# Keeping loads, transposes and small DMAs in program order, with late output weights and two more pattern buffers, in an attention kernel bound by exponentials

## The chip, the cores and the metric

The kernel runs on one core of one Trainium2 chip. The metric is the device time of one execution in microseconds (us), as the median of several executions. The kernel before took 898.3 us as the median of three runs (897.33 to 899.11). The profile of one execution is the source of everything finer than that. Its span is about 2 us shorter than the time of the run: for the kernel before 897.7 of 899.51, so the execution that was profiled is one of its slower ones. The engines go by short names: PE multiplies matrices, ACT, DVE and POOL work on elements, SP issues transfers. SBUF is the memory on the chip, PSUM the memory that PE writes its results to.

## The reference, cut to what matters

Two attention blocks, A and B, each work on 2048 rows of 512 columns with 32 heads of 16 columns, and their results stand side by side in the output.

```python
def _A_ref(x, wq, wk, wv, wo, beta):          # four segments of L = 512 rows
    ...                                        # q, k, v = x @ wq, x @ wk, x @ wv, split by head and segment
    for s in range(N):
        logits = jnp.einsum('bhqd,bhkd->bhqk', qs, ks) * scale + mask
        p = _softmax(logits, axis=-1)
        a_dot = jnp.einsum('bhqk,bhkd->bhqd', p, vs)
        pq = phi(qs)
        a_mem = ...                            # from the memory M, z of the segments before
        o = g * a_mem + (1.0 - g) * a_dot
        M = M + jnp.einsum('bhld,bhle->bhde', phi(ks), vs)
        z = z + ...
    return o @ wo

def _B_ref(x, wqkv, wo):                       # full attention over 2048 rows
    scores = jnp.einsum('bhqd,bhkd->bhqk', q, k) * Dh ** (-0.5)
    p = _softmax(scores, axis=-1)
    ...
    return o @ wo
```

Part A works on one segment after another: each needs its slice of `x`, transposed, then projections to `q`, `k` and `v`. Part B has 2048 by 2048 scores for each head, sixteen times those of one segment of A, and so most of the exponentials.

## The kernel before

ACT computes exponentials (`pT`) from score tiles that PE writes into PSUM (`s_ps`). DVE takes 500 of part B's 2048 score tiles (`v_ps`) in another way: it writes bit patterns into buffers named `vx` ("pattern buffers", 10 of them), which serve as probabilities directly; four such tiles make a block. PE multiplies both kinds by the values into `acc`. SP issues nearly all transfers, one after another.

A segment of A's input is loaded by four transposes into a buffer that exists once. The query of a unit of work (one segment of rows and one quarter of the heads) is projected into `q_ps`, cast by DVE to `qc`, and spread by head parity into `qa` (part A) or `qb` (part B): by eight small copies that SP issues when the plan finds SP free, or by two POOL instructions otherwise.

```python
    def load_xT(pool, name, ch, tag, bufs):
        t = pool.tile([P, 4, W], BF16, name=f"xT_{name}", tag=tag, bufs=bufs)
        for cc in range(4):
            nc.sync.dma_start_transpose(t[:, cc, :], xs[name][ch * W:(ch + 1) * W, cc * P:(cc + 1) * P])
        return t
    ...
        def evac():                                    # in do_q, the query projection
            qc = wk.tile([P, W], BF16, name="qc", tag="qc", bufs=2)
            pin(nc.vector.tensor_copy(qc[:], ps[:]))
            if live[0] and T["sp"] < T["dve"] + 1.0:
                for e in range(2):
                    for j in range(4):
                        r = slice(32 * j + DH * e, 32 * j + DH * e + DH)
                        nc.sync.dma_start(out=dst[r, e, :], in_=qc[r, :])
                        on_sp(0.5, T["dve"] + 0.1)
                mark(key, T["sp"] + 2.2)
            else:
                ...                                    # two POOL instructions
```

`pin` keeps an instruction where the program has it; what is not pinned may be moved by the scheduler that comes after. In the kernel before the matmuls and the work of DVE, ACT and POOL are pinned and the transfers are not.

The program plans its own order while it is written out. `T` holds a planned clock for each engine (`T["pe"]`, `T["sp"]` and so on), and the work beside the score tiles consists of "chores", each with a due place and perhaps an earliest time `after` and a condition `ok`. A chore starts only once its `after` has passed on PE's planned clock.

```python
        def startable(c):
            return ((c["after"] is None or c["after"] <= T["pe"]) and (c["ok"] is None or c["ok"]())
                    and (not c["slot"] or free_slots(T["pe"] + 0.05)))
        ...
        def seg_chores(s, rt):                         # for segment s of A and each quarter rt of the heads
            ...
            def project():
                rel = T["sp"] + 3.5
                if (s, rt) != (0, 0):
                    chore(d - LEAD, part(k()), 4, after=rel if s else ARRIVE["w1" if rt == 1 else "wk"],
                          key=("k", "a", s, rt), ok=lambda: s == 0 or ("phk", s - 1, rt) in seen)
                    chore(d - LEAD, part(q()), 4, after=rel if s else ARRIVE["w1" if rt == 1 else "wq"],
                          key=("q", "a", s, rt))
                ...
            def load():
                if s > 0:
                    xTA[s] = load_xT(wk, "a", s, "xTA", 1)
                    on_sp(4 * 1.3, T["pe"])
                ...
                project()
            if rt == 0:
                chore(d - 18, load(), 1, slot=False, ok=...)
            else:
                project()
        ...
        def unit_done(u):
            ...
            if name == "a" and ch < NSEG - 1:
                mem_chores(ch, rt)
                seg_chores(ch + 1, rt)
```

For the first quarter, `project()` is called by `load()`, so its `rel` ("the time at which the load has landed, by plan") is right. For the other quarters it is called when a unit of the segment before is done, and that can be before the load has been planned: `rel` is then a time already past.

## Time and profile before

| | kernel before |
|---|---|
| time, median of 3 runs | 898.3 us |
| span of the profiled execution | 897.7 us |
| ACT busy | 866.6 us, of it 747 exponentials with 854.9 us |
| ACT idle: first 20 us / 180 to 200 / 880 to the end / elsewhere | 8.67 / 7.30 / 10.36 / 4.74 us |

The page of a profile gives the busy time of each engine and the costliest groups of instructions. A group's row reads: line, engine, operation, output from input, count; then busy time and the mean of one in ns; then how long the engine was idle just before them and what ended most of that. Since ACT's idle time is the only thing that can shrink as long as its work stays the same, it is worth listing by stretches. The DMA issues of the kernel before, with count, size of each and median time from issue to landing, name the transfers that the change touches:

```profile
qb<-qc SPq DMA_DIRECT2D x96, 16.0 KB, 1.8
qa<-qc SPq DMA_DIRECT2D x72, 16.0 KB, 1.8
wo_a<-in_A_wo_dram SPq DMA_DIRECT2D x1, 512.0 KB, 5.0
```

So 21 query splits (168 copies in eights) go over SP's queue, and the output weights take 5.0 us to land.

### The profile page before, as it was taken

The page shows a single profiled execution, that of the slowest core. Times are in us where ns is not written, and L with a number is a line of the kernel's source. Part 1 is how long each engine was busy: PE and PEld are TensorE (multiplying, and loading weights), DVE is VectorE, ACT ScalarE, POOL GpSimd, SP SyncE. Part 2 cuts the span into 40 slices and gives each one's busy share as a digit, 9 for nine tenths or more (in the row PEclk, how much of TensorE's full clock was granted, in tenths as well). Part 3 has the DMA queues.
Part 4 walks back from the last instruction along what each step waited for, and adds up shares of the span by engine and source line. Part 5 has one row for each costly group of instructions (what it writes and reads, how often), then busy time and mean ns, then how long its engine had stood idle before and what let it go on. Part 6 is the DMA issues. An engine that isn't in the chain of part 4 may idle for free.

```text
span 897.7 us, 19235 instructions
## 1 busy us (share of the span) xinstructions
PE 863.9 (96%) x7673; PEld 258.9 (29%) x7673; DVE 796.1 (89%) x1362; ACT 866.6 (97%) x777; POOL 130.8 (15%) x295
## 2 busy tenths in 40 slices
PE   9999999979999999999999999999999999999996
PEld 3322332312323232222232322323222322222222
DVE  4786699959998998989989999999999999999994
ACT  6999999969999999999999999999999999999995
POOL 7710300310202003030110302002030300000000
PEclk9999999979999999999999999999999999999998
DMA  9600000200001201000000210000000000000000
GB/s 194 140 10 12 24 18 9 48 18 7 15 6 19 60 23 28 7 7 13 2 19 2 42 37 12 3 1 7 1 8 1 19 24 13 1 2 1 1 2 29
DMA packets 48181, 19.85 MB, mean 22 GB/s; under 512 B 37200, under 2 KB 48080, under 8 KB 48080
## 3 DMA queue, kind: packets, MB, share of 16 engines
q1 hardware_dynamic: 46736, 17.99, 9.1%
q8 instruction: 62, 1.02, 0.5%
q10 hardware_dynamic: 1344, 0.52, 0.2%
q14 instruction: 39, 0.32, 0.1%
HBM read 4.20 MB, written 4.19 MB: 9 GB/s over the span
## 4 chain that ended last, share of the span: by engine, by line
ACT 25%; PE 21%; issue 9%; DVE 5%; POOL 0%; DVEq 0%; ACTq 0%
ACT pT L893 24%; PE acc L117 11%; PE s_ps L117 6%; PE v_ps L117 2%; DVE vx L966 2%; DVE vx L982 2%; PE o_ps L117 1%; DVE tT L382 1%; ACT ex L307 0%; POOL pT L903 0%; PE l_ps L117 0%; PE q_ps L117 0%; DVE OT_b L430 0%; DVE rsum L405 0%; DVE osb L1264 0%
## 5 line engine op out<-in xcount | busy, mean ns | idle before, releaser
L893 ACT ACTIVATE pT<-s_ps 128x1536 bf16<-128x1536 f32 x747 | 854.9, 1289 | 13.0 <-PE s_ps L117 8.8
L966 DVE TENSOR_SCALAR vx<-v_ps 128x512 uint16<-128x512 f32 x500 | 328.4, 685 | 26.8 <-PE v_ps L117 21.6
L117 PE MATMUL s_ps<-qb,KB 32*128 32x512 bf16 x1548 | 249.4, 384 | 8.2 <-ACT pT L893 4.0
L982 DVE TENSOR_SCALAR vx<-vx 128x2048 uint16<-128x2048 uint16 x375 | 248.9, 693 | 5.0 <-PE v_ps L117 3.2
L117 PE MATMUL v_ps<-qb,KB 32*128 32x512 bf16 x500 | 181.8, 382 | 2.0 <-DVE vx L966 0.9
L117 PE MATMUL acc<-vx,VB 128*32 128x512 f16 x2000 | 180.8, 384 | 2.0 <-DVE vx L982 0.7
L903 POOL TENSOR_SCALAR_AFFINE_SELECT pT<-pT 128x256 bf16<-128x256 bf16 (+2 forms) x241 | 105.8, 469 | 481.8 <-ACT pT L893 481.3
L117 PE MATMUL acc<-pT,VB 128*32 128x512 bf16 x1548 | 151.6, 389 | 0.0
L117 PEld LDWEIGHTS <-KB 32*128 32x128 bf16 x2048 | 82.8, 91 | 237.1 <-issue 230.2
L117 PE MATMUL acc<-zeros 128*128 128x512 bf16 x395 | 135.4, 389 | 0.0
L117 PEld LDWEIGHTS <-VB 128*32 128x32 bf16 x3548 | 73.4, 94 | 165.6 <-issue 154.1
L117 PE MATMUL s_ps<-qa,kA 32*128 32x384 bf16 (+3 forms) x512 | 53.3, 299 | 5.3 <-ACT pT L893 3.0
L117 PEld LDWEIGHTS <-zeros 128*128 128x128 bf16 x417 | 34.2, 98 | 82.5 <-issue 77.2
L382 DVE STREAM_TRANSPOSE tT<-acc 128x512 f32<-128x512 f32 x64 | 44.9, 704 | 12.8 <-PE acc L117 12.4
L117 PE MATMUL acc<-pT,vA 128*32 128x256 bf16 (+3 forms) x512 | 33.3, 306 | 0.3 <-POOL pT L903 0.2
L117 PEld LDWEIGHTS <-kA 32*128 32x128 bf16 x512 | 17.8, 91 | 45.3 <-issue 42.3
L272 DVE CAST qc<-q_ps 128x512 bf16<-128x512 f32 x28 | 19.1, 684 | 6.8 <-PE q_ps L117 6.6
L117 PE MATMUL q_ps<-xT_a,w_a 128*128 128x512 bf16 x64 | 19.8, 386 | 5.0 <-DMA xT_a<-in_A_x_dram 5.0
L460 DVE CAST osb<-o_ps 128x512 bf16<-128x512 f32 x28 | 19.1, 683 | 4.6 <-PE o_ps L117 4.1
L416 POOL TENSOR_TENSOR tN<-tT,rsum 128x512 bf16<-128x512 f32 x1 | 1.4, 1368 | 130.1 <-DVE rsum L405 130.1
L117 PE MATMUL k_ps<-xT_a,w_a 128*128 128x512 bf16 x64 | 19.8, 398 | 0.0
L117 PE MATMUL o_ps<-wo_a,OT_a 128*128 128x512 bf16 x64 | 18.8, 383 | 0.3 <-DVE vx L966 0.2
(94 smaller groups left out, 409.7 us busy)
## 6 DMA issues: line engine op xcount, KB each, us to landing
out_dram<-osb SPq DMA_DIRECT2D x30, 128.0 KB, 1.7
w_b<-in_B_wqkv_dram SPq DMA_DIRECT2D x3, 512.0 KB, 6.0
qb<-qc SPq DMA_DIRECT2D x96, 16.0 KB, 1.8
qa<-qc SPq DMA_DIRECT2D x72, 16.0 KB, 1.8
phk<-phkT SPq DMA_TRANSPOSE x48, 2.4
w_a<-in_A_wv_dram SPq DMA_DIRECT2D x1, 512.0 KB, 5.1
wo_a<-in_A_wo_dram SPq DMA_DIRECT2D x1, 512.0 KB, 5.0
wo_b<-in_B_wo_dram SPq DMA_DIRECT2D x1, 512.0 KB, 4.9
```

The lines of the kernel that those rows point to most:

```text
L117: return pin(nc.tensor.matmul(out, lhsT, rhs, **k))
L272: pin(nc.vector.tensor_copy(qc[:], ps[:]))
L382: pin(nc.vector.transpose(st["tT"][:, e].rearrange("p c d -> p (c d)"), acc[:]))
L416: pin(eng.tensor_tensor(o, tT[:, :, :, 0:DH], rr.to_broadcast(bc), op=ALU.mult))
L460: pin(nc.vector.tensor_copy(osb[:], ps[:]))
L893: pin(nc.scalar.activation(pT[:, 0:n, :], pt[:, 0:n, :], ACT.Exp, scale=SCALE))
L903: pin(nc.gpsimd.affine_select(out=blk, in_=blk, compare_op=ALU.is_ge, fill=0.0, base=0, pattern=[[0, len(sls)], [1, P]], channel_multiplie ...
L966: pin(nc.vector.tensor_scalar(x[:, j, :], vt[:], XSCALE, float(LADDER[0]), ALU.mult, ALU.add))
L982: pin(nc.vector.tensor_scalar(p[:], x[:], float(off - LADDER[0]), 32767.0, ALU.add, ALU.min))
```

## The change

The intent, as read from the diff, is to remove the hole at 180 to 200 us and to use SBUF better. Every transfer is pinned, so that SP issues in the order of the program. The output weights no longer occupy buffers of their own from the start: they are loaded later into two of the pattern buffers, and these become 12 in place of 10, so that two more are there early.

```diff
-VBUFS = 10
+VBUFS = 12
...
-    def load_wo(pool, name, eng):
-        t = pool.tile([P, NRT, D], BF16, name=f"wo_{name}", tag=f"wo_{name}")
-        eng.dma_start(out=t[:], in_=wos[name].rearrange("(rt p) n -> p rt n", p=P))
+    def load_wo(pool, name, tag, bufs):
+        t = pool.tile([P, NRT, D], BF16, name=f"wo_{name}", tag=tag, bufs=bufs)
+        pin(nc.sync.dma_start(out=t[:], in_=wos[name].rearrange("(rt p) n -> p rt n", p=P)))
...
-            nc.sync.dma_start_transpose(t[:, cc, :], xs[name][ch * W:(ch + 1) * W, cc * P:(cc + 1) * P])
+            pin(nc.sync.dma_start_transpose(t[:, cc, :], xs[name][ch * W:(ch + 1) * W, cc * P:(cc + 1) * P]))
...
-                        nc.sync.dma_start(out=dst[r, e, :], in_=qc[r, :])
+                        pin(nc.sync.dma_start(out=dst[r, e, :], in_=qc[r, :]))
...            (the same pin on the loads of weights and beta, the phk transposes and the output)
-        woA = load_wo(big, "a", nc.sync)
-        woB = load_wo(big, "b", nc.sync)
+        wo = {}
...
+        def wo_loads():
+            for name in "ab":
+                vlive[0] += 1
+                wo[name] = load_wo(wk, name, "vx", VBUFS)
+                on_sp(0.55, T["pe"])
+            wo["at"] = T["sp"] + 4.0
+            return
+            yield
+        chore(60, wo_loads(), 1, slot=False, ok=lambda: vlive[0] + 2 < VBUFS and place() > 40)
...
-                    chore(at + 8 + 4 * sb, do_out(mp, wk, name, ot, woA if name == "a" else woB, ch, sb, gone))
+                    chore(at + 8 + 4 * sb, do_out(mp, wk, name, ot, wo, ch, sb, gone),
+                          ok=lambda: wo.get("at", 1e9) < T["pe"])
```

More of the change, by code (lines that the diff above doesn't have):

```diff
@@ L191, in load_beta @@
     def load_beta():
-        nc.sync.dma_start(out=beta_a[:], in_=A_beta.partition_broadcast(P))
+        pin(nc.sync.dma_start(out=beta_a[:], in_=A_beta.partition_broadcast(P)))
     def spread_beta():
@@ L221, in load @@
         def load(eng, i, lo=0, hi=D):
-            eng.dma_start(out=t[i][:, :, lo:hi],
-                          in_=srcs[i][:, lo:hi].rearrange("(cc p) n -> p cc n", p=P))
+            pin(eng.dma_start(out=t[i][:, :, lo:hi],
+                              in_=srcs[i][:, lo:hi].rearrange("(cc p) n -> p cc n", p=P)))
         return t, load
-    def load_wo(pool, name, eng):
-        t = pool.tile([P, NRT, D], BF16, name=f"wo_{name}", tag=f"wo_{name}")
-        eng.dma_start(out=t[:], in_=wos[name].rearrange("(rt p) n -> p rt n", p=P))
+    def load_wo(pool, name, tag, bufs):
+        t = pool.tile([P, NRT, D], BF16, name=f"wo_{name}", tag=tag, bufs=bufs)
+        pin(nc.sync.dma_start(out=t[:], in_=wos[name].rearrange("(rt p) n -> p rt n", p=P)))
         return t
@@ L337, in move @@
             for kb in range(4):
-                nc.sync.dma_start_transpose(ph[:, kb, :], pk[:, kb * P:(kb + 1) * P])
+                pin(nc.sync.dma_start_transpose(ph[:, kb, :], pk[:, kb * P:(kb + 1) * P]))
             on_sp(4 * SPTRANS, T["dve"] + 0.1)
@@ L451, in do_out @@
     def do_out(mp, wk, name, ot, wo, ch, sb, then=None):
+        if isinstance(wo, dict):
+            wo = wo[name]
         ps = palloc(mp, [P, D], "o_ps")
@@ L461, in evac @@
             r0 = ch * W + sb * P
-            nc.sync.dma_start(out=out2[r0:r0 + P, col0[name]:col0[name] + D], in_=osb[:])
+            pin(nc.sync.dma_start(out=out2[r0:r0 + P, col0[name]:col0[name] + D], in_=osb[:]))
             on_sp(0.55, T["dve"] + 0.1)
@@ L1227, in partial @@
             for rt in range(NRT - 1):
-                mm(t, ot[:, rt, sb * P:(sb + 1) * P], woB[:, rt, :], start=(rt == 0), stop=False,
+                mm(t, ot[:, rt, sb * P:(sb + 1) * P], wo["b"][:, rt, :], start=(rt == 0), stop=False,
                    skip_group_check=True)
@@ L1248 @@
                                     tN[:, 4 * sb:4 * sb + 4, :].rearrange("p c d -> p (c d)")))
-            mm(ps[sb], ot[:, NRT - 1, sb * P:(sb + 1) * P], woB[:, NRT - 1, :], start=False, stop=True,
+            mm(ps[sb], ot[:, NRT - 1, sb * P:(sb + 1) * P], wo["b"][:, NRT - 1, :], start=False, stop=True,
                skip_group_check=True)
@@ L1293, in exact_problem @@
                 ld(nc.sync, i)
-            wo = load_wo(big, name, nc.sync)
+            wo = load_wo(big, name, "wo", 1)
             xT = [load_xT(big, name, ch, f"xT{ch}", 1) for ch in range(4)]
```

## The prediction

> **What bounds the kernel now.** I read the page's busy line first, then the row of the costliest group, then all engines in stretches of 20 us, and last the one stretch that stood out, in 2 us steps and in order of time.
>
> ```profile
> PE 863.9 (96%) x7673; PEld 258.9 (29%) x7673; DVE 796.1 (89%) x1362; ACT 866.6 (97%) x777; POOL 130.8 (15%) x295
> L893 ACT ACTIVATE pT<-s_ps 128x1536 bf16<-128x1536 f32 x747 | 854.9, 1289 | 13.0 <-PE s_ps L117 8.8
> ```
>
> ACT is busy 866.6 of 897.7 us, 854.9 of it in the 747 exponentials `pT`. PE at 96% is partly filler (395 matmuls on `zeros`). So the span is ACT's work plus ACT's idle time. The stretches say where that lies (columns: stretch, PE, PEld, DVE, ACT, POOL busy, granted clock, DMA share, GB/s):
>
> ```profile
> 160.00:180.00 20.00, 19.17 (x175) 6.71 (x173) 18.90 (x37) 20.00 (x19) 8.58 (x19) 1.00 0.27 53
> 180.00:200.00 20.00, 14.96 (x92) 3.35 (x92) 10.19 (x18) 12.70 (x13) 3.67 (x4) 0.74 0.09 20
> 200.00:220.00 20.00, 19.47 (x174) 5.78 (x174) 19.61 (x34) 19.66 (x19) 0.00 (x0) 1.00 0.03 8
> ```
>
> Over all stretches ACT's idle time is 8.67 us in the first 20 us, 7.30 in 180 to 200, 10.36 from 880 to the end, and 4.74 spread over the other 840 us. With 866.63 busy that is the 897.7. So only 7.3 us lie in one hole, and PE, DVE and ACT all stop in it. What stops them, by the waits and the time line:
>
> ```profile
> PE q_ps L117 <- DMA xT_a<-in_A_x_dram: 5.0, 1, 5.0
> 174.84 3.74 SPq L234 DMA_TRANSPOSE xT_a<-in_A_x_dram  x3
> 178.68 4.96 SPq L277 DMA_DIRECT2D qa<-qc  x8
> 180.30 0.82 PE L117 MATMUL q_ps<-xT_a,w_a 128*128 128x512 bf16 x3
> 183.68 1.26 SPq L234 DMA_TRANSPOSE xT_a<-in_A_x_dram  x1
> 186.48 0.59 PE L117 MATMUL q_ps<-xT_a,w_a 128*128 128x512 bf16 x1 [5.04 <-DMA xT_a<-in_A_x_dram]
> 188.63 1.45 ACT L893 ACTIVATE pT<-s_ps 128x1536 bf16<-128x1536 f32 x1 [5.02 <-PE s_ps L117]
> ```
>
> The four transposes that load the third segment of A's input (`xT_a`) stand in SP's queue as three, then eight small copies `qa<-qc` of the query split, then the fourth. PE does three matmuls of a query projection, then waits for the fourth transpose, and everything behind it in PE's order waits too. The clock falls as well:
>
> ```profile
> 186.00:188.00 2.00, 1.52 (x12) 0.17 (x11) 0.89 (x2) 0.00 (x0) 0.11 (x1) 0.50 0.00 0
> 192.00:194.00 2.00, 2.00 (x9) 0.24 (x6) 0.49 (x1) 0.63 (x2) 0.00 (x0) 0.50 0.10 17
> 194.00:196.00 2.00, 2.00 (x19) 0.49 (x18) 1.90 (x5) 1.95 (x2) 0.00 (x0) 0.80 0.09 16
> ```
>
> So the hole is 5.02 us without matmuls plus about 2.3 us (7.30 - 5.02) of small gaps while PE runs at half clock up to about 194.8.
>
> **What the Trainium skill says.** "Perfetto Trace Analysis", Identifying the Most-Contended Engine: occupancy is a fair measure for ACT, matmul busy share is not one for PE; the trace agrees, since ACT's gaps account for the span. The same page, DMA Instruction — HWDGE (DVE, Sync): the sequencer waits for semaphores, generates descriptors, and only then is free; the movement itself lies outside the profiled slice. The trace agrees: a transpose held SP 1.26 us and PE resumed 186.48 - 183.68 = 2.8 us after its start. "DMA: Bandwidth & Descriptors", Issuing engines are not separate DMA queues, calls the sequencer's issue time "usually small relative to the DMA itself"; here it is not: eight `qa` copies hold SP 4.96 us and each lands in 1.8. "TensorE: Matmul & The Clock Gate", What's actually happening: an idle window of about 3.4 us halves PE's clock, and some 3.4 us of sustained work restores it. Here 5.0 us of idleness halved it, but it came back only some 8 us after PE resumed.
>
> **The change, part by part.** (1) ACT and DVE work: counted over the two built programs, both have the same instructions on these engines, 747 exponentials and 125 pattern blocks (500 evacuations) included. The two extra pattern buffers let blocks start earlier, but take nothing off ACT: 0 us of work. (2) Three query splits move from 24 SP copies (-16 `qa`, -8 `qb`) to 6 POOL instructions of 0.7 to 0.9 us; POOL is at 15% and their readers come tens of tiles later: 0. (3) The two output weight loads leave the front of SP's queue (1.44 + 0.51 us of issue at 33.7 to 35.7), where ACT idles only 0.27 us between 20 and 40: at most 0.3 us. Their late place is 8 score tiles ahead of the first reader, some 9 us at 1.14 us a tile (854.9 / 747), against 5.0 us to land: no wait. (4) Program order on SP. This should close the hole, and what matters is what that order is. In the changed program it reads: eight `qa<-qc`, then all four transposes of the third `xT_a`. The last reader of the old `xT_a`, which frees the buffer, is the same matmul whose result the eight copies carry. So the first three transposes lose the place ahead of the copies that the scheduler had given them. And PE's order has the first matmul on the new `xT_a` two score tiles after that last reader; before it came five tiles after, and the one on the fourth transpose six.
>
> Clocked from t = end of that last reader (174.8 before), by durations of the trace:
> - DVE's cast of `qc` ends at 0.8 (before: 175.61); copies 0.9 to 5.9 (4.96); transposes start at 5.9, 7.15, 8.4, 9.65 (1.26 each) and land 2.8 later: 8.7, 9.95, 11.2, 12.45. In the kernel before the four landed at about 2.8, 4.1, 5.3 and 11.6.
> - PE reaches its first matmul on them at about 1.8: two score tiles behind exponentials of 1.36 and 0.95, and eight small matmuls (0.45). It waits 6.9 us. ACT has two exponentials and one `ex` (0.7) in store and runs dry at 3.9, as before 2.15 us after PE stopped (181.46, 183.61).
> - PE's order is two of the four matmuls, a score tile, the other two. The score tile follows the second landing: 9.95 + 0.45 + 0.6 at half clock, ACT resumes at 11.1. Gap 7.15.
> - The next tile waits for the fourth landing, 12.45, one matmul (0.45), twelve column matmuls (1.45 at the pace of 187.00 to 187.97 for eight) and its own 0.6: 14.95, while ACT ended at 12.55. Gap 2.4.
> - Then PE is at half clock and dense with projections: gaps of about 0.45, 0.7 and 0.9, until the clock returns near 18 to 21; I take 1.8 for the three.
>
> Sum 11.4 us of idle ACT in place of 7.3: +4.1. The other five late `xT` loads of the changed program have their first reader 10 tiles or more after the issue, longer than 5.0 + 2.8 us, so no second hole. 898.3 + 4.1 = 902.4 us.
>
> **The rivals.** First, the intent: the order closes the hole. Then 898.3 - 7.3 = 891.0. For it speaks that no copies stand between transposes any more; against it that they now stand ahead of all four. It needs PE to reach the reader some 5 to 10 us later than its order suggests. Second, half of it: PE comes late by a few us because DVE or a buffer holds it, and the longer queue and the shorter wait cancel: 896 to 899. Third, a new wait at the split `qa` of a later unit: its copies now follow the two weight loads, and its first reader comes 8 tiles after its cast (9.2 us, against 4.96 + 1.8 + 0.8). Tight but enough; if a weight load waits for its buffer, up to 3 us more: 905. Fourth, the drift of the 4.74 us of small gaps under a changed interleaving: 2 us either way.
>
> **Range and chances.** Gain beyond 2% means under 880.3, but ACT's work with today's head and tail alone is 866.6 + 8.7 + 10.4 = 885.7: excluded unless the work shrinks, and it doesn't. Loss beyond 2% means over 916.3, that is a second hole of twice the size: unlikely. I give the longer hole 75%, cancelling 12%, the closed hole 8%, worse 5%. Predicted 902.4, range 897 to 907; faster 0.01, same 0.96, slower 0.03.
>
> **What would show it.** Right: in the changed kernel's time line eight `qa` copies end just before four `xT_a` transposes of 1.26 us in a row, near 175 to 186 us; PE `q_ps` waits for the `xT_a` DMA 6 to 8 us in total, in more than one piece; ACT idles 10 to 13 us in the 20 us around it; the exponentials stay at 747 and about 855 us; first and last 20 us are unchanged. Wrong: ACT busy 20 of 20 us there (the closed hole), or a wait of a score tile for `qa<-qc`, or of `o_ps` for the weights, or a DVE or POOL group grown by more than 3 us.

## The result, and the profile after

The changed kernel took 901.12 us (median of four runs, 900.9 to 901.68), against 898.02 us (four runs, 897.33 to 899.11) for the kernel before on the same chip. The ratio is 1.0034, with a 95% interval of 1.0017 to 1.0052. Here and below a ratio is the mean time of one kernel's fast runs over the mean of the other's fast runs of the same rounds, so it is not quite the ratio of the medians quoted; in the experiments below, the first execution of each kernel, the profiled one, is left out of it. All runs quoted here count as fast.

The page of the changed kernel, its busy line and the row of the costliest group:

```profile
PE 850.7 (95%) x7617; PEld 258.8 (29%) x7677; DVE 792.7 (88%) x1362; ACT 866.0 (96%) x777; POOL 131.2 (15%) x301
...
L903 ACT ACTIVATE pT<-s_ps 128x1536 bf16<-128x1536 f32 x747 | 854.2, 1294 | 16.2 <-PE s_ps L117 14.1
```

The work is the same: 747 exponentials, 854.2 us. What changed is the idle time before them, 16.2 us, of which 14.1 ended with a score tile of PE, in place of 13.0 and 8.8. The stretches of the changed kernel (PE, PEld, DVE, ACT, POOL busy, granted clock, DMA share, GB/s) say where:

```profile
160.00:180.00 20.00, 16.31 (x142) 5.84 (x143) 16.47 (x35) 19.08 (x18) 7.65 (x18) 1.00 0.22 37
180.00:200.00 20.00, 14.00 (x72) 3.31 (x73) 5.71 (x10) 10.08 (x10) 4.51 (x6) 0.66 0.15 33
200.00:220.00 20.00, 18.59 (x173) 5.45 (x173) 19.09 (x33) 19.84 (x19) 0.00 (x0) 1.00 0.06 12
```

ACT idles 0.92 + 9.92 = 10.84 us in the first two, where it idled 7.30 before. The mean granted clock of the second stretch is 0.66 in place of 0.74. The row of the waits for the same transfer, and then the time line of the changed kernel around it (start, duration, engine, line, operation, count, and in brackets the idle time before it with what ended it):

```profile
PE q_ps L117 <- DMA xT_a<-in_A_x_dram: 8.5, 4, 6.9
```

```profile
176.29 4.94 SPq L277 DMA_DIRECT2D qa<-qc  x8
181.33 5.12 SPq L234 DMA_TRANSPOSE xT_a<-in_A_x_dram  x4
184.04 0.61 PE L117 MATMUL q_ps<-xT_a,w_a 128*128 128x512 bf16 x1 [6.91 <-DMA xT_a<-in_A_x_dram]
...
186.46 1.45 ACT L903 ACTIVATE pT<-s_ps 128x1536 bf16<-128x1536 f32 x1 [7.38 <-PE s_ps L117]
...
187.97 0.59 PE L117 MATMUL q_ps<-xT_a,w_a 128*128 128x512 bf16 x1 [0.69 <-DMA xT_a<-in_A_x_dram]
...
190.11 1.02 ACT L903 ACTIVATE pT<-s_ps 128x1024 bf16<-128x1024 f32 x1 [1.69 <-PE s_ps L117]
```

The reader should see four things. The eight `qa` copies end just before four transposes in a row. PE waits for each of the four landings, not for one: 8.5 us in 4 waits in place of 5.0 in 1. The first wait begins at 177.1 us, 1.7 us after the last matmul on the old buffer ended (175.47). And ACT's gaps, 7.38, 1.69 and after these 0.49, 1.11 and 0.17, sum to 10.84.

The span grew from 897.7 to 899.2 us. By ACT's idle time the hole gave +3.54, the first 20 us -0.20 (8.47 idle), the stretch from 880 us -0.53 (9.83), all other idle time -0.70 (4.04), and the busy time -0.6: together +1.5. One execution each is profiled, the kernel before in a slower one than its median, as said above; the medians of the runs differ by 3.1.

The transfers, from the DMA issues of the changed kernel:

```profile
qb<-qc SPq DMA_DIRECT2D x88, 16.0 KB, 1.8
qa<-qc SPq DMA_DIRECT2D x56, 16.0 KB, 1.8
```

Three splits have moved to POOL (24 copies fewer), and no row of the waits shows anything waiting for the output weights, which are now issued at about 76 us.

### The profile page after: what moved, and what is told of

It reads as the page before. It is cut to its first block, busy times and chain, and to the rows that moved or that the text cites. A ratio compares the mean times of both kernels' runs of the same rounds, so it can differ in the third digit from the quotient of the medians.

```text
span 899.2 us, 19135 instructions
## 1 busy us (share of the span) xinstructions
PE 850.7 (95%) x7617; PEld 258.8 (29%) x7677; DVE 792.7 (88%) x1362; ACT 866.0 (96%) x777; POOL 131.2 (15%) x301
## 2 busy tenths in 40 slices
DMA packets 47412, 19.45 MB, mean 22 GB/s; under 512 B 36816, under 2 KB 47312, under 8 KB 47312
## 4 chain that ended last, share of the span: by engine, by line
PE 23%; ACT 20%; issue 7%; DVE 4%; DMA 0%; DVEq 0%; SPq 0%; ACTq 0%
ACT pT L903 19%; PE acc L117 13%; PE s_ps L117 7%; PE v_ps L117 2%; DVE vx L976 1%; DVE vx L992 1%; PE o_ps L117 1%; DVE tT L382 0%; PE q_ps L117 0%; DMA phk<-phkT 0%; DMA out_dram<-osb 0%; DVE osb L462 0%; PE l_ps L117 0%; ACT ex L307 0%; DVE tN L428 0%
## 5 line engine op out<-in xcount | busy, mean ns | idle before, releaser
L903 ACT ACTIVATE pT<-s_ps 128x1536 bf16<-128x1536 f32 x747 | 854.2, 1294 | 16.2 <-PE s_ps L117 14.1
L992 DVE TENSOR_SCALAR vx<-vx 128x2048 uint16<-128x2048 uint16 x375 | 245.8, 683 | 2.6 <-PE acc L117 1.2
L117 PE MATMUL v_ps<-qb,KB 32*128 32x512 bf16 x500 | 179.6, 381 | 2.3 <-DVE osb L462 0.6
L913 POOL TENSOR_SCALAR_AFFINE_SELECT pT<-pT 128x256 bf16<-128x256 bf16 (+2 forms) x241 | 102.8, 456 | 532.4 <-ACT pT L903 531.4
L117 PE MATMUL s_ps<-qa,kA 32*128 32x512 bf16 (+3 forms) x512 | 53.2, 299 | 5.7 <-ACT pT L903 3.6
L117 PE MATMUL q_ps<-xT_b,w_b 128*128 128x512 bf16 x53 | 18.2, 410 | 1.1 <-issue 0.7
L117 PE MATMUL k_ps<-xT_a,w_a 128*128 128x512 bf16 x58 | 17.8, 382 | 0.6 <-issue 0.6
```

The lines of the kernel that those rows point to most:

```text
L117: return pin(nc.tensor.matmul(out, lhsT, rhs, **k))
L903: pin(nc.scalar.activation(pT[:, 0:n, :], pt[:, 0:n, :], ACT.Exp, scale=SCALE))
L913: pin(nc.gpsimd.affine_select(out=blk, in_=blk, compare_op=ALU.is_ge, fill=0.0, base=0, pattern=[[0, len(sls)], [1, P]], channel_multiplie ...
L992: pin(nc.vector.tensor_scalar(p[:], x[:], float(off - LADDER[0]), 32767.0, ALU.add, ALU.min))
```

## The experiments

Each was run in five rounds, and all results were correct. The theory (A): the hole comes from the plan, which lets PE start a query projection on an input segment right behind the last reader of the old one, without knowing that the new one is not there; the rest of the change sets only how long that wait is: what stands ahead of the transposes in SP's queue, and how soon PE's order comes to the projection. The rival at first (B): SP's order alone made the difference. A second one (C): part of the later gaps is the granted clock, not the transfer.

### The changed kernel again

No edit; it gives the spread against the same runs of the kernel before that the next three are compared with.

> The changed kernel once more, on the same chip as the other runs of this call. All theories: about 901 us, ratio to the kernel before 1.002 to 1.005, ACT idle 10 to 11.5 us between 160 and 200 us (it was 10.84 in its first trace, 7.30 in the kernel before).

Measured: 901.54 us (899.7 to 902.02) against 897.52 (9 runs), ratio 1.0038 [1.0024, 1.0052]. The hole in its profile is 1.11 + 9.37 = 10.48 us. The result repeats, with some 0.4 us of scatter in the hole. This profile also has 1.95 us of idle ACT at 510 to 530 us, where the first profile of the kernel had 0.45.

### Order alone

The kernel before with `pin` around every transfer, and nothing else:

```diff
-            nc.sync.dma_start_transpose(t[:, cc, :], xs[name][...])
+            pin(nc.sync.dma_start_transpose(t[:, cc, :], xs[name][...]))
...            (and so for the copies, loads and outputs)
```

> The kernel before with program order on SP's queue alone: old buffers, old weight loads. The built program equals the kernel before on PE, DVE, ACT and POOL; only SP's order differs (eight copies, then all four transposes of the third xT_a). Theory A (what costs is how far behind the last reader PE reaches the new xT_a, and that is set by the interleaving, not by the queue): PE still comes five to six tiles after the last reader, so it waits about 3 us for the first and 1 to 2 for the others; hole 7.5 to 8.5 us, time 897.5 to 900. Rival B (the order of the queue alone makes the whole loss): hole about 11 us, 901 to 902. Rival C (the intent: program order on the queue closes the hole): under 893.

Measured: 898.47 us (897.62 to 900.48) against 897.52, ratio 1.0013 [0.9999, 1.0027]. The time line of this run:

```profile
175.03 4.94 SPq L277 DMA_DIRECT2D qa<-qc  x8
180.07 5.12 SPq L234 DMA_TRANSPOSE xT_a<-in_A_x_dram  x4
...
186.59 1.02 ACT L893 ACTIVATE pT<-s_ps 128x1024 bf16<-128x1024 f32 x1 [4.50 <-PE s_ps L117]
```

SP's order is that of the changed kernel, and PE's program is that of the kernel before. Three of the four transposes now start some 5 us later (the first at 180.07 in place of 174.84), and yet the hole is 6.95 us, no larger than 7.30 (and below the 7.5 to 8.5 expected). PE waits 4.5 us in three pieces in place of 5.0 in one. The last transpose leaves SP at 180.07 + 5.12 = 185.19 us, and in the kernel before at 183.68 + 1.26 = 184.94: what ends the hole is the end of the whole sequence of copies and transposes, and that hardly depends on the order within it (counted from the end of the last reader, 174.21 us here and 174.82 before, it is 0.9 us later). Rivals B and C are out: order alone neither closes the hole nor brings the whole loss. It does not show any loss for certain, since its interval includes 1, but one of up to 0.27% is not excluded.

### Buffers and late weights alone

The changed kernel with `pin` taken off every transfer, so the scheduler may again move them.

```diff
-            pin(nc.sync.dma_start_transpose(t[:, cc, :], xs[name][...]))
+            nc.sync.dma_start_transpose(t[:, cc, :], xs[name][...])
...            (and so for the others)
```

> The changed kernel without program order on its transfers: twelve pattern buffers and late weights stay. The built program equals the changed one on PE, DVE, ACT and POOL; SP's order is two transposes, eight copies, two transposes. Theory A: PE comes two tiles after the last reader, gets the first two transposes after a short wait, then waits for the third and fourth; hole about 10 to 11 us in two pieces, the first about 1 us and the second about 7.5; time 900 to 901.5. Rival B: hole as in the kernel before, 7.3 us, 898. A third view, that the buffers help by themselves: under 897.

Measured: 899.27 us (897.95 to 900.38), ratio 1.0018 [1.0005, 1.0032]. From its time line:

```profile
178.26 4.97 SPq L280 DMA_DIRECT2D qa<-qc  x8
183.28 2.56 SPq L237 DMA_TRANSPOSE xT_a<-in_A_x_dram  x2
...
189.55 1.02 ACT L906 ACTIVATE pT<-s_ps 128x1024 bf16<-128x1024 f32 x1 [7.07 <-PE s_ps L120]
```

The scheduler again puts transposes ahead of the copies, but only two of the four, at 175.73 us. PE waits 0.95, 5.64 and 0.78 us. The hole is 0.68 + 8.67 = 9.35 us, a little below the 10 to 11 that I expected, and so is the time. The new interleaving of PE's work is therefore the larger part of the growth of the hole: +2.05 us without the order, and 1.1 to 1.5 us more with it (10.48 and 10.84). The times don't settle the shares: 1.0018 here and 1.0013 for order alone have intervals that overlap. This run holds both the two early buffers and the late weights; which of them moved PE's order is not separated.

### The reader told when the load has landed

The changed kernel with a correction of the plan alone. A projection may not start before its load has been planned, and its earliest time is set to the planned landing:

```diff
-        u_at, nmem, nproj = [0], {}, {0: 2}
+        u_at, nmem, nproj, xin = [0], {}, {0: 2}, {0: 0.0}
...
-                          key=("k", "a", s, rt), ok=lambda: s == 0 or ("phk", s - 1, rt) in seen)
+                          key=("k", "a", s, rt), ok=lambda: s in xin and (s == 0 or ("phk", s - 1, rt) in seen))
...
-                          key=("q", "a", s, rt))
+                          key=("q", "a", s, rt), ok=lambda: s in xin)
...
                     on_sp(4 * 1.3, T["pe"])
+                    xin[s] = T["sp"] + 3.5
+                    for c in chores:
+                        if c["key"] is not None and c["key"][1:3] == ("a", s):
+                            c["after"] = xin[s]
```

> The changed kernel with one correction in the kernel's own planner: the k and q projections of a later segment are held until the time planned for that segment's xT_a load, in place of a time taken before the load was planned. SP's order stays (copies, then four transposes); the first reader of the third xT_a moves from two score tiles after the last reader to fourteen. ACT and DVE have the same instructions. Theory A: no wait for the xT_a transfer, hole under 1 us, clock stays at 1.0; time 901.1 - 10.8 + up to 1 = 890 to 891.5, faster than both kernels. Rival (the loss is not this wait, the time only moves to another one): 897 or more.

Measured: 890.56 us (890.31 to 892.87), ratio 0.9925 [0.9911, 0.9938] to the kernel before. Its stretches:

```profile
160.00:180.00 20.00, 18.81 (x162) 6.60 (x163) 16.69 (x36) 20.00 (x19) 7.66 (x18) 1.00 0.21 37
180.00:200.00 20.00, 19.19 (x163) 6.27 (x167) 17.68 (x29) 20.00 (x20) 3.15 (x4) 1.00 0.17 37
```

ACT is busy 20.00 of 20 us in both, at full clock, and no wait for `xT_a` is left. SP's order is unchanged: the copies at 176.29 us and the four transposes at 181.34, almost to the hundredth where they were in the changed kernel. So nothing had to be done about the queue; the transfer had been early enough for the work, and only the place of the projections in PE's order was wrong. This is the strongest run for theory A. The two parts of the correction, the condition and the new time, were tested together. A second buffer for `xT_a`, which would let the load start before the last reader is done, was not tried.

### The copies twice

In the changed kernel, the eight copies of that one query are issued twice; the planned cost of each is halved, so that the plan stays as it was.

```diff
-                for e in range(2):
+                for e in [0, 1] * (2 if key == ("q", "a", 1, 3) else 1):
...
-                        on_sp(0.5, T["dve"] + 0.1)
+                        on_sp(0.25 if key == ("q", "a", 1, 3) else 0.5, T["dve"] + 0.1)
```

> The changed kernel with the eight copies ahead of the third xT_a load issued twice (the same data to the same place; result unchanged, all other engines' programs equal). Theory A: the four transposes start 8 x 0.62 = 4.96 us later, PE waits 11.9 us for the first, and the whole of it goes into the time: hole 15.5 to 16.5 us, time 905.5 to 907. Rival (SP's issue time lies beside other work, the wait is for the movement of the data): under 903.

Measured: 905.69 us (905.35 to 906.15) against 898.14 (11 runs), ratio 1.0083 [1.0068, 1.0098]. In the time line:

```profile
175.97 10.00 SPq L277 DMA_DIRECT2D qa<-qc  x16
186.07 5.12 SPq L234 DMA_TRANSPOSE xT_a<-in_A_x_dram  x4
...
191.34 1.45 ACT L903 ACTIVATE pT<-s_ps 128x1536 bf16<-128x1536 f32 x1 [12.58 <-PE s_ps L117]
```

The hole is 16.0 us. Another 5.06 us of issue made the first gap 5.2 us longer (12.58 in place of 7.38) and left the later ones nearly alone (1.60, 0.49, 1.33, 0.32). Issue time ahead of the transposes goes into the time one for one, or nearly: the ratios differ by 0.0045 to 0.0049 from the changed kernel's, which is 4.0 to 4.4 us.

### No copies

In the changed kernel, that one query is split by two POOL instructions in place of eight copies, with the plan's clock for SP unchanged.

```diff
-                        pin(nc.sync.dma_start(out=dst[r, e, :], in_=qc[r, :]))
+                        if key != ("q", "a", 1, 3):
+                            pin(nc.sync.dma_start(out=dst[r, e, :], in_=qc[r, :]))
+                        elif j == 0:
+                            pin(nc.gpsimd.tensor_scalar(dst[:, e, :], qc[:], par[:, e:e + 1], 0.0, ALU.mult, ALU.add))
```

> The changed kernel with no copies ahead of that load: this one query split is done by two POOL instructions, the plan's clocks are left as they were, so PE, DVE and ACT have the same programs. Theory A: the transposes start at the last reader's end and land 2.8, 4.1, 5.3 and 6.6 us after it, PE at 1.8 waits about 1 us three times; hole 2.5 to 4.5 us, time 893 to 895. If only the late plan of the reader counted and not the queue, the hole would stay over 7 us and the time over 897.

Measured: 895.1 us (894.79 to 896.05), ratio 0.9968 [0.9955, 0.9982]. From its time line and its stretches:

```profile
176.13 5.12 SPq L234 DMA_TRANSPOSE xT_a<-in_A_x_dram  x4
180.00:200.00 20.00, 18.22 (x112) 4.65 (x113) 10.90 (x18) 15.78 (x15) 4.52 (x6) 0.83 0.10 21
```

PE waits 3.6 us in four pieces of at most 1.4. ACT's gaps are 1.78, 1.79, 0.49, 0.65 and 0.17, 4.88 us in all, a little more than the 2.5 to 4.5 expected; the clock fell here too (mean 0.83). The hole shrank by 6.0 us against the changed kernel, and the ratios differ by 6 us too. So even with a free queue the plan's mistake costs some 4 to 5 us (the hole, and 0.9968 against 0.9925): a transpose took 1.26 us to issue and nearly 3 to land.

### The correction in the kernel before

The correction above in the kernel before, with nothing else.

> The kernel before with the planner's correction alone: old queue order, ten pattern buffers, early weights. The planner then gives one block less to DVE (124 of 125), so ACT has two exponentials of 2 banks more, about 1.9 us. Theory A: 898.0 - 7.3 + 1.9 = 892.6, between 891.5 and 894; so most of the gain needs neither the program order nor the buffers. Rival (the order on the queue is needed for it): over 896.

Measured: 895.38 us (894.26 to 896.14), ratio 0.997 [0.9956, 0.9984]. This is a miss: I had expected 892.6. The hole at 180 to 200 us is gone (19.93 us busy of 20), but a second one has come at 500 to 520 us:

```profile
500.00:520.00 20.00, 15.14 (x134) 4.00 (x137) 14.66 (x28) 14.97 (x15) 0.00 (x0) 0.91 0.21 56
505.49 0.69 DVE L460 CAST osb<-o_ps 128x512 bf16<-128x512 f32 x1 [4.08 <-DMA out_dram<-osb]
```

SP had two transposes, eight `qb` copies and two more transposes in its queue, and then four outputs; DVE waited 4.08 us for the buffer of one output (`osb`). The plan also came out with 749 exponentials in place of 747 (124 pattern blocks and not 125), but their busy time, 854.7 us, is that of the kernel before within 0.3 us, so it is not this that was lost. The correction changes the whole plan, and what closing the old hole gave was mostly spent again in the new one.

### The correction without the order

The corrected changed kernel with `pin` taken off the transfers.

> The corrected changed kernel without program order on its transfers (programs of PE, DVE, ACT, POOL equal to the corrected one). Theory A: the reader comes fourteen tiles, some 16 us, after the last reader, so either order of the queue is in time: 890 to 891.5, same as with order. Rival (program order is worth something by itself once the reader is told): 892 or more.

Measured: 891.26 us (889.46 to 892.22), ratio 0.9922 [0.9907, 0.9938]: the same as with the order. With the reader told, program order on SP is worth nothing measurable in this kernel.

### The correction and the order, with the old buffers

The kernel before with the pins and the correction: whether the order closes the second hole of the correction in the kernel before, where copies stood between transposes.

> The kernel before with the planner's correction and program order on SP's queue, but ten pattern buffers and early weights: the programs of PE, DVE, ACT and POOL equal those of the corrected kernel with the old rest (895.4), only SP's order differs. That kernel had a second hole of about 5 us near 500 us, where output transfers stood behind a split load (two transposes, eight copies, two transposes) and DVE waited 4.1 us for an output buffer. Theory: program order puts the outputs at their planned place, that hole goes: 890 to 892. Rival (that hole belongs to the plan of the other engines, not to the queue): 894 or more.

Measured: 896.06 us (895.51 to 897.72) against 897.65 (11 runs), ratio 0.9984 [0.9972, 0.9996]. A miss for the theory that the order would close it; the rival held. From the time line, SP and DVE:

```profile
493.74 5.46 SPq L277 DMA_DIRECT2D qb<-qc  x8
499.30 5.12 SPq L234 DMA_TRANSPOSE xT_b<-in_B_x_dram  x4
504.54 3.09 SPq L462 DMA_DIRECT2D out_dram<-osb  x4
...
506.58 0.69 DVE L460 CAST osb<-o_ps 128x512 bf16<-128x512 f32 x1 [4.42 <-DMA out_dram<-osb]
```

Three outputs that DVE had ready in their buffers at 496.9 to 501.6 us stand behind 10.7 us of copies and transposes (493.74 to 504.42); there are three `osb` buffers, the next output has none, and DVE, pinned in its order, stops for 4.42 us. In the corrected changed kernel the same stretch has the outputs between the other transfers (two at 498.47 us, right after the copies) and ACT busy 19.98 of 20 us. So the rest of the change is worth something after all, some 5 us by the two ratios (0.9925 and 0.9984), but by another plan of the work near 500 us, not by the order.

### The first wait filled

The changed kernel with 28 matmuls on zeros (which add nothing) in front of the waiting projection, so that PE does not idle there.

```diff
+                if (s, rt) == (2, 1):
+                    for _ in range(28):
+                        pin(nc.tensor.matmul(accs[cur[0]][:], zeros[:, 0, :], zcols, start=False, stop=False,
+                                             skip_group_check=True))
                 yield from do_q(...)
```

> The changed kernel with 28 more zero matmuls of 0.216 us (about 6.0 us) just before the first matmul that waits for the third xT_a, the plan's clocks left as they are: PE works where it waited, so its clock should not be halved. Theory: the wait for the transfer stays (first ACT gap about 6.9 us in place of 7.4), but the gaps after it, 3.5 us in the changed kernel, fall to about 1; granted clock 1.0; hole 7.5 to 8.5 us; time 898 to 899.5. Rival (the later gaps come from the order of the work and not from the clock): hole over 10 us, time over 900.5.

Measured: 900.16 us (898.81 to 900.93) against 897.65, ratio 1.0026 [1.0013, 1.0038]. The hole is 10.92 us. This did not tell what it should: the later gaps stayed (1.99, 0.49, 1.17, 0.17), and the clock fell all the same, only later. Four stretches of 1 us, columns as before:

```profile
185.00:186.00 1.00, 0.52 (x4) 0.10 (x3) 0.00 (x0) 0.00 (x0) 0.00 (x0) 1.00 0.51 116
186.00:187.00 1.00, 0.32 (x4) 0.19 (x2) 0.00 (x0) 0.71 (x1) 0.00 (x0) 1.00 0.28 61
187.00:188.00 1.00, 0.23 (x1) 0.00 (x0) 0.00 (x0) 1.00 (x2) 0.00 (x0) 0.61 0.39 86
188.00:189.00 1.00, 0.89 (x5) 0.14 (x8) 0.27 (x1) 0.25 (x1) 0.00 (x0) 0.50 0.00 0
```

PE was busy until 183.29 us and then had four waits of 0.68 to 0.96 us for the landings, the fourth from 187.24. The clock halved within the microsecond from 187, although no single wait reached 1 us.

### All waits filled

As before, with 31, 4, 2 and 4 such matmuls in front of the four matmuls of the projection.

```diff
+                    for fill in (31, 4, 2, 4):
+                        for _ in range(fill):
+                            pin(nc.tensor.matmul(accs[cur[0]][:], zeros[:, 0, :], zcols, start=False, stop=False,
+                                                 skip_group_check=True))
+                        ...                           # then the next matmul of do_q
```

> What it separates: how much of the hole is the halved clock. In the run with 28 zero matmuls the fill covered only the first wait; the matmul unit was then busy 0.39, 0.52, 0.32 and 0.23 us in the four microseconds of the later landings, and the clock halved at about 187.5. Here 31 zero matmuls stand before the first query matmul on the third input segment, and 4, 2 and 4 before the second, third and fourth, in the changed kernel, so that the unit stays busy until the fourth landing. Theory (the first gap is the transfer, the later gaps are the half clock): granted clock 1.00 in 180 to 200 us; first gap of the exponentials 7.0 to 7.3 us, unchanged; second gap 0.9 to 1.3 in place of 1.7 to 2.0; third and fourth (0.49, 1.1) gone or under 0.2; hole 8.8 to 9.5 us in place of 10.8; time 1.3 to 2.0 us below the changed kernel's, 899 to 900. Rival (the later gaps come from the order of the work and the fourth landing, and the clock costs next to nothing): clock 1.00 but hole 10.3 or more, time as the changed kernel, 901. If the clock still falls, the run says nothing of this.

Measured: 898.9 us (898.54 to 900.75) against 897.18 (9 runs), ratio 1.0027 [1.0013, 1.004]. Its stretch, and ACT in its time line:

```profile
180.00:200.00 20.00, 19.45 (x122) 6.22 (x120) 7.99 (x14) 12.72 (x12) 4.51 (x6) 1.00 0.17 36
```

```profile
186.01 1.45 ACT L915 ACTIVATE pT<-s_ps 128x1536 bf16<-128x1536 f32 x1 [7.12 <-PE s_ps L117]
189.07 3.39 ACT L915 ACTIVATE pT<-s_ps 128x1024 bf16<-128x1024 f32 x3 [1.09 <-PE s_ps L117]
```

The clock stayed at 1.00. The first gap is unchanged, the second is 1.09, and the two after it have become back-to-back exponentials with one gap of 0.17. ACT idles 1.11 + 7.28 = 8.39 us in 160 to 200, so by this one profile 2.1 to 2.4 us of the 10.48 and 10.84 were the halved clock and 8.4 the transfer. In the profile theory C is shown with about that size. In the times it is less certain: by the medians the run is 1.7 us above the kernel before, where the changed kernel was 3.1 and 4.0 above, but by the ratios the gain is 0.0007 to 0.0011, 0.6 to 1.0 us, which the intervals don't separate from none; of the five executions three took 898.5 to 898.9 us, the profiled one among them, and two 900.6 to 900.8, so something that the hole doesn't explain varies too. PE reads 19.45 us busy of 20 here with ACT at 12.72: a reader who goes by PE's busy share alone would not see the hole at all.

### The corrected kernel again

> The corrected changed kernel again on this call's chip, to compare it with the corrected kernel with old buffers: 890 to 891.5. If the buffers and late weights are worth nothing by themselves, the two are within 1 us; its one dip of the clock near 545 us (2.2 us of idle ACT in the first trace) should come in some executions only.

Measured: 891.21 us (889.63 to 892.68) against 897.65, ratio 0.9924 [0.991, 0.9939]. With 0.9925 in its first run, and level with the run without pins (0.9922), this is the best version of all: faster than the kernel before by 0.75% and, as 0.9925 / 1.0038 shows, than the changed kernel by 1.1%. Its profile has a drop of the clock at 545 to 552 us, with 2.15 us of idle ACT from 540 to 560, as its first run had (2.22) and the profile without pins had not, though PE's program is the same there. It follows on three microseconds in which PE was busy 0.79, 0.40 and 0.80 us (542 to 545; 0.77, 0.42 and 0.80 in the first run), and no transfer is waited for. In the profile without pins these were 0.92, 0.27 and 0.80, and the clock held.

The order need not be the reason. The six executions here fall into two groups: 889.63 to 890.12 us with a mean clock of 0.996 or 0.997, and 892.29 to 892.68 with 0.994, as expected of a dip that comes in some executions only. The run without pins has both kinds too (889.46 to 890.62 and 891.91 to 892.22). Both profiles with the dip were taken of an execution of the slower group (892.87 and 892.68), and the one without it of the faster (889.79). What decides it is open.

### The runs in one table

| ratio to the kernel before | old buffers, weights early | new buffers, weights late |
|---|---|---|
| scheduler's order | 1 | 1.0018 |
| program order | 1.0013 | 1.0034, 1.0038 |
| scheduler's order, reader told | 0.9970 | 0.9922 |
| program order, reader told | 0.9984 | 0.9925, 0.9924 |

In each pair of rows the program order is the slower or level (by 0.0013 and about 0.0018 without the correction, 0.0014 and 0.0003 with it); no pair alone is clear of the noise, but in none did the order help.

## Why the prediction was right, and where not

**The work and the parts that cost nothing.** Steps 1 to 3 held: 747 exponentials with 854.2 us, the same DVE work, no wait for a split on POOL, none for the output weights, and at most a few tenths in the first 40 us (the first 20 lost 0.20 us of idle time). The rivals of a new wait at `qa` and of a second hole did not come.

**The longer hole.** The sequence was as described: copies at 176.29, transposes at 181.33, and PE at the projection 1.7 us after the last reader (predicted 1.8). PE's first wait was 6.91 us (predicted 6.9). By terms:

| gap of ACT | predicted | measured |
|---|---|---|
| first | 7.15 | 7.38 |
| second | 2.4 | 1.69 |
| three small ones | 1.8 | 0.49 + 1.11 + 0.17 = 1.77 |
| sum | 11.4 | 10.84 |
| growth over 7.3 | +4.1 | +3.5 |

The term that was mis-sized is the second gap. ACT resumed 10.99 us after the last reader (predicted 11.1), but the exponential was followed by an `ex` of 0.62 us on the key side, which I had not counted: ACT was busy to 188.42 us in place of 188.0, and the next tile came at 190.11 in place of 190.4. So ACT's second gap was 0.71 us short of the prediction, and the hole 0.56. Of the rest of the difference between 902.4 and 901.12, 0.28 us is the base (898.3 of three runs, 898.02 of four), and 0.4 us is within the scatter of the runs. In the two profiles the first and last stretches, the small gaps and the busy time together gave back 2 us, but the profiled execution of the kernel before was itself 1.5 us over its median, so that this was the drift of the fourth rival is not shown.

**What was attributed wrongly.** The prediction put the loss under program order and gave the buffers "0 us of work". The work is indeed unchanged, but the runs show that order alone costs nothing that can be told from zero (1.0013), and that the interleaving which comes with the buffers and late weights is what brings PE to the projection earlier and lengthens the hole by 2.05 us even without the order (1.0018 in time). The sentence on PE's order (two tiles after the last reader in place of five) was the heart of the matter, and belonged to another part of the change than the one it stood under. Its "half of it" rival (queue and wait cancel) is what order alone did.

**A loose reading.** Where the prediction says of the issue time "here it is not" (small beside the transfer), it sets the issue of eight copies (4.96 us) against the landing of one (1.8 us). One copy holds SP 0.62 us. What counted is that the eight issues stand one after another ahead of the transposes, and the run with doubled copies shows that.

**What was not asked.** The prediction took the plan as given and reckoned its consequence. It did not ask why PE's program reaches a projection before its load has been issued in full, in both kernels. That question led to the stale `after`, and to a gain of 0.75% where the change gave a loss of 0.34%.

## What to carry to other kernels

When one engine carries the kernel, list its idle time by stretches and go to the one hole; then ask of the waiting instruction whether its data is late or its place in the order is early, because the second may be mended in the plan alone. Reordering the queue did not help here, since the last transfer of the sequence left SP at nearly the same time in either order (184.94 and 185.19 us); telling the planner when the load lands removed the whole hole with the transfers unmoved. Look at the whole span afterwards: in the kernel before, the same correction opened a second hole of 5 us near 500 us. Where a program plans its own order, check each "ready at" time for when it was computed: one taken before the load is planned is silently wrong, and one change elsewhere can make it cost more.

## What the Trainium skill lacked or had wrong

- "DMA: Bandwidth & Descriptors", Issuing engines are not separate DMA queues: it calls the time to initiate a transfer "usually small relative to the DMA itself". Here one 16 KB copy held SP 0.62 us (4.94 / 8) and landed in 1.8 us, so about a third. And the issues add up on one queue: eight held back the transposes by 4.94 us, sixteen by 10.00, and ACT's gap grew by 5.2 us.
- "TensorE: Matmul & The Clock Gate", What's actually happening: its table gives an idle window of about 3.4 us as the condition for the halved clock. In the run with 28 fillers it halved in the microsecond from 187 after PE had been busy 0.28, 0.39, 0.52 and 0.32 us in the four before (mean 0.38), with no wait over 0.96 us; in the corrected kernel it fell after 0.77, 0.42 and 0.80, and after 0.79, 0.40 and 0.80. The page's section A second HAM failure mode: psum-queue depth-cycling speaks of such short idle times, but gives no busy share. At a mean of 0.66 over three microseconds the clock fell in two profiles and held in one (0.92, 0.27, 0.80).
- The same table gives about 3.4 us of sustained work for the return, and the section adds that the window is free-running; so up to two windows, some 6.8 us (an estimate from its figure), would fit. In the changed kernel PE was busy with small breaks from 187.97 us, and the clock was back within the microsecond from 193, some 5 to 6 us later, which fits. In the kernel before PE was busy without a break from 187.00 us, and the clock was still at 0.50 in the microsecond from 193 and came back in the one from 194: 7 us or more, which does not.
